# A second rounding moves from ScalarE to VectorE, a state update is cut into quarters of TensorE's columns, and the order of issue is written anew

## The chip, the cores and the metric

The kernel runs on one core of one Trainium2 chip. The core has five engines that run side by side and wait for each other through semaphores: TensorE (PE) for matrix products, VectorE (DVE) and ScalarE (ACT) for elementwise work, GpSimd (POOL) and SyncE (SP), which here issues the transfers. TensorE writes its results to PSUM, from where VectorE and ScalarE read them; all other tiles lie in SBUF. The metric is the device time of one execution in microseconds, the lower the better.

## The reference

Two stages in float32. The first is a gated linear attention over 4 batches, 8 heads, 768 positions and a head dimension of 40, given as a recurrence over positions:

```python
for t in range(S):
    m_new = np.maximum(f_gate[:, :, t] + m, i_gate[:, :, t])
    f_stab = np.exp(f_gate[:, :, t] + m - m_new)
    i_stab = np.exp(i_gate[:, :, t] - m_new)
    m = m_new
    C = f_stab * C + i_stab * outer(v_t, k_t)
    n = f_stab * n + i_stab * k_t
    y[:, :, t] = sigmoid(o_gate_t) * (C @ q_t) / max(|n . q_t|, 1)
```

(shapes of the broadcasts left out). Its output, laid out as 3072 tokens of 320 numbers, goes through a two-layer MLP with a hidden width of 2048:

```python
h = x @ w_in
sp = softplus(h)
g = h * erf(sp)
return g @ w_out
```

## The kernel before

**Attention.** The 768 positions are cut into 6 chunks of 128. One attention step takes one chunk of one batch, so there are 24 steps; step s has chunk s // 4 and batch s % 4. Inside a step the positions of the chunk are handled with matrix products, and what came before the chunk is carried in a state per batch (`state`, one 104-row tile: even heads in rows 0 to 39, odd heads in rows 64 to 103). `pe`, `ex`, `sel` make the decay factors (TensorE, exponential on ScalarE, causal select on GpSimd), `S` the products of k and q, `w` their product with the factors. `ph` (L613 to L624) makes the numerators and denominators: it adds products with the state (L619) and with the chunk's own values (L623), all of them with a stationary operand cut into four slices of 32 columns. `pk` (L628 to L633) makes the update of the state: for every head one matmul with 128 rows, a stationary operand of 40 columns (the keys) and 41 moving columns (the weighted values); its result lies in rows 0 to 39 or 64 to 103 of PSUM. `sa`, `sk0`, `sk1` then scale the state and add the update on VectorE. The last chunk (steps 20 to 23) has no `pk`, `sa` or `sk`. `den`, `yg`, `y`, `tr`, `xh`, `xl` finish the step's output, transpose it and split it into a rounded part and a rest. From step 4 on, `klo` and `qlo` (L531, L539) do the same split for k and q, whose parts are stacked by transfers (`stk`). A float32 matmul shows up as two records in the profile, and so do its weight loads.

**MLP.** Products in the rounded float32 form are fast on TensorE but lose bits, so each operand is split in two (rounded value and rest) and three of the four products are added. 48 groups are worked off; a group takes 256 tokens (the steps of two batches) and 512 of the 2048 hidden columns, so each pair of steps has four groups. A group's parts: `up0` to `up3` (L817, 32 matmuls into two PSUM tiles), `a` and `hb` (L833, L827) read them on ScalarE, a chain of ScalarE functions (`a2`, `sq`, `b`, `w`: L837, L841, L846, L858) and VectorE operations (`ah`, `ab`, `wh`: L850, L854, L862) approximates the activation, and the result stands in `hb`. Then `gh` (L867) rounds `hb` into its own tile and `gl` (L872) makes the rest, `hb` minus `gh`, on VectorE. `dn0` to `dn7` (L886, L887, L889) multiply both by the output weights, 24 matmuls; after the fourth group of a token block `o0`, `o1` copy the sums out and store them. `hb`, the two work tiles, `gh` and `gl` have two buffers each, so two groups can be between `up` and `dn` on VectorE and ScalarE.

**Weights.** Both weight matrices arrive packed as 64-bit numbers and are decoded once, in the first 100 us, in 26 pieces (`decode`, L698 to L731), using the tiles of the MLP and of attention as room.

**Order.** Nothing in the kernel is a loop over time. Every part is put on a list with a due time, which is the start of its unit (a step, a group, a chunk of gates, a decoded piece) plus an offset for the part from a table (`ATT_FIRST`, `ATT_NEXT`, `ATT` for steps 0 and 1, 2 and 3, and the rest; `MLP_FIRST`, `MLP_NEXT`, `MLP`, `MLP_END` for group 0, 1 to 3, 4 to 45, 46 and 47). The list is sorted by due time (L919) and the instructions are issued in that order; each engine takes its own in that order, one after the other. Due times set only this order, they aren't times of the chip.

Of the kernel before, what the change touches and what calls it, by code (L numbers as in the profile page):

```python
# [46 lines left out]

SETUP = {'setup': -813.8827,  # L50
    'rhs0': -388.4174,
    'rhs1': -3.147,
    'sel': -262.192}
GATE = {'load': -186.9771,
    'scan': -141.2439,
    'g': -125.5882,
    'sum': -102.716,
    'exp': -93.5536,
    'part0': -68.8941,
    'part1': -61.4429,  # L60
    'part2': -57.2668,
    'rhs': -56.4504}
ATT_FIRST = {'load': -208.3528,
    'loadv': -198.2534,
    'khi': -56.4056,
    'qhi': -409.6725,
    'klo': 276.929,
    'qlo': 281.4546,
    'stk0': -218.0962,
    'stk1': 40.1164,  # L70
    'rows': -216.9163,
    'pe0': -116.0988,
    'pe1': -102.408,
    'ex0': -111.8168,
    'ex1': -96.8755,
    'sel0': -98.0918,
    'sel1': -96.6502,
    'S0': -96.3594,
    'S1': -62.8169,
    'vg0': -88.4143,  # L80
    'vg1': -92.2802,
    'w0': -75.0031,
    'w1': -56.2056,
    'th': -55.2198,
    'pq': -206.9946,
    'qa': -240.2257,
    'pk': -77.3251,
    'ph': -43.1067,
    'sa': -140.0059,
    'sk0': -67.4399,  # L90
    'sk1': -74.5887,
    'den': -36.2945,
    'yg': -37.4924,
    'y': -12.5989,
    'tr': -3.0494,
    'xh': -2.6837,
    'xl': 1.504}
ATT_NEXT = {'load': -149.0934,
    'loadv': -49.2114,
    'khi': -8.6302,  # L100
    'qhi': 90.9856,
    'klo': 33.5053,
    'qlo': -184.8211,
    'stk0': 14.6892,
    'stk1': 195.1025,
    'rows': -194.6127,
    'pe0': -78.3983,
    'pe1': -89.2505,
    'ex0': -66.02,
    'ex1': -71.4482,  # L110
    'sel0': -51.4336,
    'sel1': -67.3981,
    'S0': -67.0238,
    'S1': -35.5688,
    'vg0': -41.9021,
    'vg1': -31.4188,
    'w0': -35.7311,
    'w1': -27.6603,
    'th': -39.2487,
    'pq': -219.6827,  # L120
    'qa': -104.0043,
    'pk': -12.9812,
    'ph': 3.8011,
    'sa': -212.9552,
    'sk0': 5.0577,
    'sk1': -4.6847,
    'den': 6.0789,
    'yg': 12.8402,
    'y': 20.8014,
    'tr': 23.7301,  # L130
    'xh': 34.3967,
    'xl': 38.586}
ATT = {'load': -35.6274,
    'loadv': -44.8494,
    'khi': -27.6843,
    'qhi': -24.58,
    'klo': -24.3722,
    'qlo': -23.7744,
    'stk0': -19.1999,
    'stk1': -17.7163,  # L140
    'rows': -57.5337,
    'pe0': -18.8968,
    'pe1': -34.5401,
    'ex0': -12.4881,
    'ex1': -29.3698,
    'sel0': -6.6822,
    'sel1': -26.618,
    'S0': -10.7393,
    'S1': -4.962,
    'vg0': -5.5713,  # L150
    'vg1': -10.3348,
    'w0': -2.8802,
    'w1': -3.1066,
    'th': 5.0062,
    'pq': -28.6139,
    'qa': -22.8277,
    'pk': 3.3201,
    'ph': 3.7715,
    'sa': 19.0615,
    'sk0': 25.9894,  # L160
    'sk1': 22.7007,
    'den': 6.5626,
    'yg': 8.3629,
    'y': 9.8824,
    'tr': 13.0984,
    'xh': 17.8939,
    'xl': 18.4217}
DEC = {'val': 5.6701,
    'bits': 8.8322,
    'hi': 14.5496,  # L170
    'lo': 23.4348,
    'dif': 18.0177}
MLP_FIRST = {'up0': -18.4204,
    'up1': -16.3411,
    'up2': -12.9276,
    'up3': -11.4394,
    'hb0': -6.2952,
    'a0': -14.0994,
    'hb1': -0.8876,
    'a1': -5.4375,  # L180
    'a2': 7.3924,
    'sq': 10.0013,
    'b': 12.0363,
    'ah': 16.7161,
    'ab': 19.9043,
    'w': 27.7463,
    'wh': 32.4163,
    'gh': 37.7164,
    'gl': 38.1861,
    'dn0': 42.3165,  # L190
    'dn1': 48.7899,
    'dn2': 54.3768,
    'dn3': 65.1336,
    'dn4': 42.1446,
    'dn5': 44.8041,
    'dn6': 50.2294,
    'dn7': 62.4136,
    'o0': 242.6862,
    'o1': 100.7839}
# [152 lines left out]
def tile_mlstm_moe(  # L352
# [136 lines left out]
    def attention(s):  # L489
# [123 lines left out]
        @at('ph')  # L613
        def _():
            v.ph = psum(H, V1)
            halves = [slice(32 * i, 32 * i + 32) for i in range(4)]
            for p in range(NPR):
                for ts in halves if c > 0 else ():
                    nc.tensor.matmul(v.ph[ts, 2 * p:2 * p + 2].rearrange("p h d -> p (h d)"),  # L619
                                     v.q[0:QR, p, ts], st[0:QR, p], start=True, stop=False)  # L620
                for j in range(2):
                    for ts in halves:
                        nc.tensor.matmul(v.ph[ts, 2 * p + j], v.w[j][:, p, ts], v.v1[:, 2 * p + j],  # L623
                                         start=(c == 0), stop=(c == 0 or j == 1))  # L624

        if not last:

            @at('pk')  # L628
            def _():
                v.pk = psum(NPR, V1)  # L630
                for p in range(NPR):
                    for j in range(2):
                        nc.tensor.matmul(v.pk[64 * j:64 * j + D, p], v.kn[:, 2 * p + j], v.vg[j][:, p], start=True, stop=True)  # L633
# [230 lines left out]
        @at('gh')  # L864
        def _():
            v.gh = moe.tile([128, W], F32R, name="gh")
            nc.scalar.activation(v.gh, v.hb, AF.Copy)  # L867
# [114 lines left out]
```

## Time and profile before

| | |
|---|---|
| runs | 507.61, 510.29, 510.26 us, median 510.26 |
| profiled execution | 505.95 us, span 504.1 us |
| TensorE busy | 478.0 us, 95% of the span |
| ScalarE busy | 447.7 us, 89% |
| VectorE busy | 438.5 us, 87% |
| GpSimd busy | 82.2 us, 16% |
| TensorE's granted clock over the span | 0.997 |

In the lines of the profile each group of instructions has its line of the code, its engine and operation, the tile it writes and the tiles it reads, their shapes and how many there were; behind the first bar stand the busy time in us and the mean length of one in ns, behind the second the idle time of the engine just ahead of them and what ended it. A line of the timeline begins with the start in us and the length in us. A line of a stretch has, for each engine, the us it was busy and how many instructions started. A line of the waits has the total in us, how many there were and the longest.

### The profile page before, as it was taken

The page shows a single profiled execution, that of the slowest core. Times are in us where ns is not written, and L with a number is a line of the kernel's source. Part 1 is how long each engine was busy: PE and PEld are TensorE (multiplying, and loading weights), DVE is VectorE, ACT ScalarE, POOL GpSimd, SP SyncE. Part 2 cuts the span into 40 slices and gives each one's busy share as a digit, 9 for nine tenths or more (in the row PEclk, how much of TensorE's full clock was granted, in tenths as well). Part 3 has the DMA queues.
Part 4 walks back from the last instruction along what each step waited for, and adds up shares of the span by engine and source line. Part 5 has one row for each costly group of instructions (what it writes and reads, how often), then busy time and mean ns, then how long its engine had stood idle before and what let it go on. Part 6 is the DMA issues. An engine that isn't in the chain of part 4 may idle for free.

```text
span 504.1 us, 14051 instructions
## 1 busy us (share of the span) xinstructions
PE 478.0 (95%) x5718; PEld 447.5 (89%) x5718; DVE 438.5 (87%) x677; ACT 447.7 (89%) x714; POOL 82.2 (16%) x112
## 2 busy tenths in 40 slices
PE   2877999899999999999999999999999999999996
PEld 1644779799899999999999999999999999999996
DVE  4878899898999999999998999999998977887663
ACT  4758999998989999889989899989899989989992
POOL 3203002311121121121121121121121211110000
PEclk9999999999999999999999999999999999999999
DMA  7986533324424514515505505415415325300000
GB/s 256 291 254 162 174 110 113 126 84 132 139 62 131 156 48 144 177 26 164 155 16 179 157 25 172 143 32 170 134 52 167 118 70 169 94 16 13 2 27 26
DMA packets 28315, 59.06 MB, mean 117 GB/s; under 512 B 4156, under 2 KB 8764, under 8 KB 28252
## 3 DMA queue, kind: packets, MB, share of 16 engines
q1 hardware_dynamic: 28252, 58.18, 38.0%
q8 instruction: 45, 0.74, 0.6%
q14 instruction: 18, 0.15, 0.1%
HBM read 33.40 MB, written 3.93 MB: 74 GB/s over the span
## 4 chain that ended last, share of the span: by engine, by line
PE 72%; ACT 12%; DVE 10%; issue 3%; DMA 2%; SPq 0%; POOL 0%; DVEq 0%; ACTq 0%
PE h L817 29%; PE po L886 10%; PE po L889 9%; PE po L887 9%; PE pa L578 3%; PE pa L619 3%; PE pa L623 2%; DVE bits L712 2%; PE pa L558 1%; PE pa L633 1%; DMA stk<-parts 1%; PE pa L677 1%; ACT gh L867 1%; DVE bits L711 1%; ACT bits L706 1%
## 5 line engine op out<-in xcount | busy, mean ns | idle before, releaser
L817 PE MATMUL h<-xh,wh 128*128 128x256 f32 x576 | 158.9, 285 | 0.8 <-ACT hb L827 0.8
L817 PE MATMUL h<-xl,wh 128*128 128x256 f32 x576 | 156.5, 281 | 0.2 <-DVE xl L690 0.2
L886 PE MATMUL po<-woh,gh 128*128 128x320 f32 x384 | 118.2, 318 | 1.1 <-ACT gh L867 1.1
L887 PE MATMUL po<-wol,gh 128*128 128x320 f32 x384 | 114.4, 309 | 0.0
L817 PEld LDWEIGHTS h<-xh,wh 128*128 128x128 f32 x576 | 108.5, 188 | 2.8 <-ACT hb L827 1.1
L817 PEld LDWEIGHTS h<-xl,wh 128*128 128x128 f32 x576 | 108.6, 188 | 0.7 <-DVE xl L690 0.5
L817 PE MATMUL h<-xh,wl 128*128 128x256 f32 x384 | 107.7, 281 | 0.0
L889 PE MATMUL po<-woh,gl 128*128 128x320 f32 x384 | 79.2, 326 | 0.0
L569 POOL TENSOR_SCALAR_AFFINE_SELECT dm<-dm 128x512 f32<-128x512 f32 x48 | 47.2, 986 | 169.6 <-ACT dm L565 162.0
L886 PEld LDWEIGHTS po<-woh,gh 128*128 128x128 f32 x384 | 72.2, 188 | 2.4 <-ACT gh L867 1.3
L817 PEld LDWEIGHTS h<-xh,wl 128*128 128x128 f32 x384 | 72.3, 188 | 0.0
L887 PEld LDWEIGHTS po<-wol,gh 128*128 128x128 f32 x384 | 72.2, 188 | 0.0
L872 DVE TENSOR_TENSOR gl<-hb,gh 128x1024 fp32r<-128x1024 f32 x48 | 58.7, 1222 | 12.1 <-ACT gh L867 11.6
L862 DVE SCALAR_TENSOR_TENSOR hb<-n,hb 128x1024 f32<-128x1024 f32 x48 | 58.6, 1220 | 10.2 <-ACT n L858 10.0
L854 DVE SCALAR_TENSOR_TENSOR n<-n,n 128x1024 f32<-128x1024 f32 x48 | 61.6, 1284 | 4.7
L889 PEld LDWEIGHTS po<-woh,gl 128*128 128x128 f32 x384 | 61.5, 189 | 1.0
L850 DVE SCALAR_TENSOR_TENSOR n<-n,hb 128x1024 f32<-128x1024 f32 x48 | 59.6, 1241 | 3.0 <-ACT n L841 3.0
L867 ACT ACTIVATE gh<-hb 128x1024 fp32r<-128x1024 f32 x48 | 50.8, 1058 | 11.9 <-DVE hb L862 10.3
L833 ACT ACTIVATE n<-h 128x512 f32<-128x512 f32 x96 | 57.2, 596 | 1.3 <-PE h L817 1.3
L858 ACT ACTIVATE n<-n 128x1024 f32<-128x1024 f32 x48 | 51.5, 1072 | 6.2 <-DVE n L854 6.1
L827 ACT ACTIVATE hb<-h 128x512 f32<-128x512 f32 x96 | 54.5, 603 | 1.1 <-PE h L817 0.7
L837 ACT ACTIVATE n<-n 128x1024 f32<-128x1024 f32 x48 | 51.0, 1064 | 1.0
(102 smaller groups left out, 797.6 us busy)
## 6 DMA issues: line engine op xcount, KB each, us to landing
stk<-parts SPq DMA_DIRECT2D x120, 160.0 KB
kvo<-in_kvo_dram SPq DMA_DIRECT2D x24, 484.0 KB
parts<-in_w_out_dram SPq DMA_DIRECT2D x5, 960.0 KB
parts<-in_qk_dram SPq DMA_DIRECT2D x20, 208.0 KB
q_t<-in_qk_dram SPq DMA_DIRECT2D x20, 208.0 KB
out_dram<-o_sb SPq DMA_DIRECT2D x24, 160.0 KB
stk<-in_qk_dram SPq DMA_DIRECT2D x4, 416.0 KB
hb<-in_w_in_dram SPq DMA_DIRECT2D x2, 512.0 KB
```

What stands on the lines that cost most here:

```text
L817: nc.tensor.matmul(v.h[n // 2][:, n % 2 * T:(n % 2 + 1) * T], w, m, start=(q == 0), stop=(q == len(ops) - 1))
L827: nc.scalar.activation(v.hb[:, hs], v.h[i], AF.Copy)
L833: nc.scalar.activation(v.a[:, hs], v.h[i], AF.Tanh, scale=PARAMS[0], bias=PARAMS[1])
L850: nc.vector.scalar_tensor_tensor(out=v.a, in0=v.a, scalar=PARAMS[8], in1=v.hb, op0=ALU.add, op1=ALU.mult)
L854: nc.vector.scalar_tensor_tensor(out=v.a, in0=v.a, scalar=PARAMS[9], in1=v.b, op0=ALU.mult, op1=ALU.add)
L858: nc.scalar.activation(v.a, v.a, AF.Tanh, scale=PARAMS[10], bias=PARAMS[11])
L862: nc.vector.scalar_tensor_tensor(out=v.hb, in0=v.a, scalar=1.0, in1=v.hb, op0=ALU.add, op1=ALU.mult)
L867: nc.scalar.activation(v.gh, v.hb, AF.Copy)
L872: nc.vector.tensor_tensor(v.gl, v.hb, v.gh.bitcast(F32), op=ALU.subtract)
L886: nc.tensor.matmul(po[k, b], v.gh[:, ts], woh[:, w], start=(j == 0), stop=False)
L887: nc.tensor.matmul(po[k, b], v.gh[:, ts], wol[:, w], start=False, stop=False)
L889: nc.tensor.matmul(po[k, b], v.gl[:, ts], woh[:, w], start=False, stop=(j == NFF - 1))
```

## The change

Three things. `gh` is written by a copy on VectorE instead of ScalarE. `pk` makes each head's update in two matmuls, one for the first 32 of the 40 key columns and one for the last 8, so that the four pieces of a pair of heads lie in four different quarters of TensorE's columns. And all the tables of due times are replaced. The code, and the lines of the tables for the parts named above (old and new values; all other entries and unit starts change likewise):

```diff
         @at('ph')
         def _():
             v.ph = psum(H, V1)
-            halves = [slice(32 * i, 32 * i + 32) for i in range(4)]
+            quarters = [slice(32 * i, 32 * i + 32) for i in range(4)]
...
                 v.pk = psum(NPR, V1)
                 for p in range(NPR):
-                    for j in range(2):
-                        nc.tensor.matmul(v.pk[64 * j:64 * j + D, p], v.kn[:, 2 * p + j], v.vg[j][:, p], start=True, stop=True)
+                    for d in (slice(0, 32), slice(32, D)):
+                        for j in range(2):
+                            nc.tensor.matmul(v.pk[64 * j + d.start:64 * j + d.stop, p], v.kn[:, 2 * p + j, d], v.vg[j][:, p],
+                                             start=True, stop=True)
...
         @at('gh')
         def _():
             v.gh = moe.tile([128, W], F32R, name="gh")
-            nc.scalar.activation(v.gh, v.hb, AF.Copy)
+            nc.vector.tensor_copy(v.gh, v.hb)
...
 ATT = {
-    'pk': 3.3201,
-    'ph': 3.7715,
+    'pk': 5.626,
+    'ph': 5.7311,
...
 MLP = {
-    'ah': 27.915,
-    'ab': 27.9988,
-    'w': 31.9713,
-    'wh': 35.0478,
-    'gh': 38.5408,
-    'gl': 39.3398,
+    'ah': 29.2802,
+    'ab': 31.7705,
+    'w': 36.3996,
+    'wh': 37.6271,
+    'gh': 40.7584,
+    'gl': 42.2482,
...
 MLP_END = {
-    'wh': 154.2504,
-    'gh': 203.734,
-    'gl': 213.6813,
+    'wh': 182.5552,
+    'gh': 193.2624,
+    'gl': 197.238,
...
-GROUP_EVERY = 13.6751
+GROUP_EVERY = 13.9448
```

The groups 46 and 47 are 13.94 apart in the new due times, and the order inside each table decides what stands next to what on an engine. With the new tables `up2` and `up3` of a group stand ahead of `up0` and `up1` in groups 4 to 45.

More of the change, by code (lines that the diff above doesn't have):

```diff
@@ L46 @@
 RAWS = {(0, 0): 0, (0, 1): 1, (0, 2): 2, (1, 0): 3, (1, 1): 4, (2, 0): 0, (2, 1): 1, (1, 2): 2, (3, 0): 3, (3, 1): 4}
[L50 to L156, printed above, removed]
-    'pk': 3.3201,
-    'ph': 3.7715,
[L159 to L199, printed above, removed]
@@ L323 @@
-GROUP_AT = {0: 13.6829, 1: 39.891, 2: 60.8627, 3: 80.6636, 4: 86.6757, 5: 101.5639, 6: 114.4195, 7: 128.3435, 8: 142.8737}
-STEP_AT = {0: -28.9212, 1: -10.28, 2: 33.3085, 3: 50.2721, 4: 113.3159, 5: 127.2279}
-CHUNK_AT = {0: -663.0126, 1: 103.1621}
-GROUP_EVERY = 13.6751
-STEP_BEFORE = (27.6368, 15.3426)
-CHUNK_BEFORE = 1.8963
+SETUP = {'setup': -928.5203,
+    'rhs0': -613.177,
+    'rhs1': -29.7752,
+    'sel': -139.3245}
+GATE = {'load': -224.6692,
+    'scan': -149.6546,
+    'g': -125.2395,
+    'sum': -114.6638,
+    'exp': -101.2865,
+    'part0': -90.4155,
+    'part1': -62.8155,
+    'part2': -61.5663,
+    'rhs': -57.2961}
@@ new lines @@
+ATT_FIRST = {'load': -331.2339,
+    'loadv': -344.4309,
+    'khi': -120.5911,
+    'qhi': -233.1144,
+    'klo': 528.3043,
+    'qlo': 144.2014,
+    'stk0': -167.2021,
+    'stk1': -136.2594,
+    'rows': -298.8524,
+    'pe0': -123.2307,
+    'pe1': -97.1572,
+    'ex0': -120.569,
+    'ex1': -83.4473,
+    'sel0': -120.3251,
+    'sel1': -68.3484,
+    'S0': -87.5465,
+    'S1': -88.9462,
+    'vg0': -66.8815,
+    'vg1': -59.7325,
+    'w0': -59.7409,
+    'w1': -59.4943,
+    'th': -89.0495,
+    'pq': -314.5437,
+    'qa': -252.6374,
+    'pk': -57.2283,
+    'ph': -47.6956,
+    'sa': -344.6918,
+    'sk0': -44.5247,
+    'sk1': -49.3669,
+    'den': -39.4944,
+    'yg': -36.4964,
+    'y': -34.3845,
+    'tr': -28.4862,
+    'xh': -18.7034,
+    'xl': -16.7492}
@@ new lines @@
+ATT_NEXT = {'load': -80.0853,
+    'loadv': -75.632,
+    'khi': 23.4282,
+    'qhi': 190.3113,
+    'klo': 227.0614,
+    'qlo': -11.47,
+    'stk0': -340.7925,
+    'stk1': 702.0529,
+    'rows': -149.8449,
+    'pe0': -102.6535,
+    'pe1': -109.1585,
+    'ex0': -94.484,
+    'ex1': -106.0558,
+    'sel0': -58.9502,
+    'sel1': -58.3061,
+    'S0': -52.0604,
+    'S1': -55.741,
+    'vg0': -49.5721,
+    'vg1': -48.0631,
+    'w0': -37.8363,
+    'w1': -37.3776,
+    'th': -40.0196,
+    'pq': -178.6846,
+    'qa': -249.8476,
+    'pk': -43.5433,
+    'ph': -18.413,
+    'sa': -287.4488,
+    'sk0': -28.2722,
+    'sk1': -36.3723,
+    'den': -9.2432,
+    'yg': -6.0606,
+    'y': 4.9134,
+    'tr': 10.5059,
+    'xh': 16.2231,
+    'xl': 24.6696}
@@ new lines @@
+ATT = {'load': -51.8544,
+    'loadv': -26.1722,
+    'khi': -29.3743,
+    'qhi': -25.6263,
+    'klo': -21.4556,
+    'qlo': -20.1171,
+    'stk0': -14.971,
+    'stk1': -16.124,
+    'rows': -40.8363,
+    'pe0': -32.6881,
+    'pe1': -23.6677,
+    'ex0': -13.5285,
+    'ex1': -21.1839,
+    'sel0': -8.1627,
+    'sel1': -12.8695,
+    'S0': -4.3635,
+    'S1': -8.9011,
+    'vg0': -5.0316,
+    'vg1': -10.5189,
+    'w0': 0.7873,
+    'w1': -6.0905,
+    'th': -11.0704,
+    'pq': -25.1779,
+    'qa': -13.5697,
+    'pk': 5.626,
+    'ph': 5.7311,
+    'sa': 25.3811,
+    'sk0': 30.8657,
+    'sk1': 30.9972,
+    'den': 9.8444,
+    'yg': 8.3836,
+    'y': 10.5116,
+    'tr': 12.8967,
+    'xh': 14.9233,
+    'xl': 18.4193}
@@ new lines @@
+DEC = {'val': 4.934,
+    'bits': 12.8513,
+    'hi': 14.2405,
+    'lo': 24.6701,
+    'dif': 18.3684}
+MLP_FIRST = {'up0': -33.2412,
+    'up1': -21.5925,
+    'up2': -30.8229,
+    'up3': -16.4832,
+    'hb0': -20.6038,
+    'a0': -17.9568,
+    'hb1': -13.277,
+    'a1': -12.8502,
+    'a2': -6.7127,
+    'sq': 4.2608,
+    'b': 8.3221,
+    'ah': 14.5215,
+    'ab': 20.7561,
+    'w': 27.5205,
+    'wh': 35.2425,
+    'gh': 37.3163,
+    'gl': 38.8657,
+    'dn0': 37.831,
+    'dn1': 40.5103,
+    'dn2': 43.5939,
+    'dn3': 46.3097,
+    'dn4': 37.781,
+    'dn5': 46.5542,
+    'dn6': 50.0325,
+    'dn7': 51.4237,
+    'o0': 314.4614,
+    'o1': 464.4019}
@@ new lines @@
+MLP_NEXT = {'up0': -15.5056,
+    'up1': -14.8841,
+    'up2': -13.7254,
+    'up3': -7.6506,
+    'hb0': -2.4947,
+    'a0': -2.5968,
+    'hb1': 2.7199,
+    'a1': 1.32,
+    'a2': 4.4483,
+    'sq': 10.2316,
+    'b': 12.9396,
+    'ah': 14.33,
+    'ab': 20.0619,
+    'w': 22.1515,
+    'wh': 26.9934,
+    'gh': 29.2921,
+    'gl': 33.225,
+    'dn0': 32.6721,
+    'dn1': 42.3334,
+    'dn2': 45.7049,
+    'dn3': 45.772,
+    'dn4': 32.9836,
+    'dn5': 37.9451,
+    'dn6': 38.7558,
+    'dn7': 39.3316,
+    'o0': 57.8221,
+    'o1': 42.358}
@@ new lines @@
+MLP = {'up0': 5.1145,
+    'up1': 9.1868,
+    'up2': 3.8109,
+    'up3': 4.1168,
+    'hb0': 15.1333,
+    'a0': 14.8988,
+    'hb1': 17.2812,
+    'a1': 18.7318,
+    'a2': 23.0236,
+    'sq': 23.3706,
+    'b': 28.4458,
+    'ah': 29.2802,
[4 more added lines that the diff above has]
+    'gl': 42.2482,
+    'dn0': 51.7159,
+    'dn1': 52.4413,
+    'dn2': 54.849,
+    'dn3': 55.9078,
+    'dn4': 56.0741,
+    'dn5': 58.5535,
+    'dn6': 58.6195,
+    'dn7': 61.3347,
+    'o0': 63.5735,
+    'o1': 70.265}
@@ new lines @@
+MLP_END = {'up0': 2.0072,
+    'up1': 4.5781,
+    'up2': 5.9872,
+    'up3': 6.5329,
+    'hb0': 15.6252,
+    'a0': 14.3867,
+    'hb1': 24.6476,
+    'a1': 19.8713,
+    'a2': 19.9417,
+    'sq': 25.1194,
+    'b': 27.988,
+    'ah': 88.4738,
+    'ab': 97.2004,
+    'w': 97.695,
+    'wh': 182.5552,
+    'gh': 193.2624,
+    'gl': 197.238,
+    'dn0': 205.9226,
+    'dn1': 213.8546,
+    'dn2': 214.3087,
+    'dn3': 214.5545,
+    'dn4': 297.4067,
+    'dn5': 298.0492,
+    'dn6': 298.9531,
+    'dn7': 300.5958,
+    'o0': 277.4824,
+    'o1': 359.6294}
@@ new lines @@
+LOAD = {(0, 0): -333.1427,
+    (0, 1): -79.9756,
+    (0, 2): -166.6898,
+    (1, 0): -28.1903,
+    (1, 1): -127.0378,
+    (2, 0): -12.0649,
+    (2, 1): 2.2675,
+    (1, 2): -32.2837,
+    (3, 0): -170.9967,
+    (3, 1): -76.6308,
+    ('o', 0): -627.3454,
+    ('o', 3): -478.9457,
+    ('o', 6): 3.2127,
+    ('o', 9): -56.1129,
+    ('o', 12): -230.6654,
+    ('o', 15): 19.4224}
+DECODE = {('i', 0, 0): -103.7423,
+    ('i', 0, 1): -54.8351,
+    ('t', 0): -65.3981,
+    ('i', 1, 0): -10.1182,
+    ('i', 1, 1): -67.8849,
+    ('o', 0): -167.113,
+    ('o', 1): -174.1159,
+    ('o', 2): -145.6058,
+    ('o', 3): -122.2135,
+    ('i', 2, 0): 8.6447,
+    ('i', 2, 1): 14.8529,
+    ('t', 1): -13.5021,
+    ('i', 3, 0): -83.4714,
+    ('i', 3, 1): -31.1617,
+    ('o', 4): -149.4123,
+    ('o', 5): -126.2123,
+    ('o', 6): 45.9593,
+    ('o', 7): 50.9311,
+    ('o', 8): 59.2719,
+    ('o', 9): -31.1749,
+    ('o', 10): 36.9086,
+    ('o', 11): 29.6144,
+    ('o', 12): -103.0389,
+    ('o', 13): -83.6161,
+    ('o', 14): -45.5832,
+    ('o', 15): 69.6967}
@@ L331, in group_at @@
+GROUP_AT = {0: 15.4252, 1: 40.0088, 2: 58.3328, 3: 78.2519, 4: 82.944, 5: 100.075, 6: 114.9869, 7: 128.343, 8: 145.1279}
+STEP_AT = {0: -32.7155, 1: -12.8846, 2: 29.2965, 3: 56.5819, 4: 109.4769, 5: 123.9825}
+CHUNK_AT = {0: -764.7163, 1: 83.9429}
+GROUP_EVERY = 13.9448
+STEP_BEFORE = (29.9975, 17.6754)
+CHUNK_BEFORE = -8.7286
 def group_at(g):
@@ L615, in _ @@
             v.ph = psum(H, V1)
-            halves = [slice(32 * i, 32 * i + 32) for i in range(4)]
+            quarters = [slice(32 * i, 32 * i + 32) for i in range(4)]
             for p in range(NPR):
-                for ts in halves if c > 0 else ():
+                for ts in quarters if c > 0 else ():
                     nc.tensor.matmul(v.ph[ts, 2 * p:2 * p + 2].rearrange("p h d -> p (h d)"),
@@ L621, in _ @@
                 for j in range(2):
-                    for ts in halves:
+                    for ts in quarters:
                         nc.tensor.matmul(v.ph[ts, 2 * p + j], v.w[j][:, p, ts], v.v1[:, 2 * p + j],
```

114 lines of the change are left out of this document (removed).

## The prediction

> **What bounds the kernel now.** I read the busy totals of the page first, then the busy time by stretch, then the waits of VectorE in the long middle stretch.
>
> ```profile
> PE 478.0 (95%) x5718; PEld 447.5 (89%) x5718; DVE 438.5 (87%) x677; ACT 447.7 (89%) x714; POOL 82.2 (16%) x112
> ...
> PE 72%; ACT 12%; DVE 10%; issue 3%; DMA 2%; SPq 0%; POOL 0%; DVEq 0%; ACTq 0%
> ```
>
> ```profile
> core 0: us, PE busy (x) PEld busy (x) DVE busy (x) ACT busy (x) POOL busy (x), PEclk, DMA share, GB/s
> 0.00:100.00 100.00, 80.53 (x760) 61.61 (x761) 82.48 (x162) 79.99 (x159) 17.83 (x38) 0.98 0.63 186
> 100.00:382.00 282.00, 279.67 (x3725) 270.46 (x3724) 266.17 (x413) 260.25 (x400) 53.56 (x62) 1.00 0.37 114
> 382.00:456.00 74.00, 74.00 (x919) 72.23 (x918) 62.59 (x81) 70.05 (x108) 10.80 (x14) 1.00 0.34 103
> 456.00:485.00 29.00, 29.00 (x225) 29.00 (x224) 18.12 (x17) 28.00 (x39) 0.00 (x0) 1.00 0.03 9
> 485.00:504.10 19.10, 14.78 (x99) 14.16 (x98) 9.10 (x8) 9.44 (x13) 0.00 (x0) 1.00 0.07 26
> ```
>
> The stretches matter more than the totals. From 100 to 485 TensorE is the bound (279.67 of 282, then all of it). From 100 to 382, where attention steps run beside the MLP, VectorE is close behind: 266.17 of 282. After 382 it has room (62.59 of 74, 18.12 of 29), because the last chunk needs no update of the state and no further gates. Before 100 no engine is full. The whole-kernel share of 87% for VectorE hides this, and the change puts work on VectorE.
>
> ```profile
> DVE kvo L661 <- ACT den L656: 4.3, 8, 1.3
> DVE gl L872 <- ACT gh L867: 2.2, 4, 0.6
> DVE hb L862 <- ACT n L858: 1.8, 4, 0.4
> DVE n L850 <- ACT n L841: 0.7, 3, 0.2
> DVE dm L592 <- PE pa L578: 0.5, 2, 0.2
> ```
>
> These are all of VectorE's waits for others from 100 to 382: 4.3 + 2.2 + 1.8 + 0.7 + 0.5 = 9.5 us. The other idle time, 282 - 266.17 - 9.5 = 6.3 us, lies between its own dependent instructions and stays whatever the others do. So VectorE has 9.5 us to give away there.
>
> **Part 1: gh moves from ScalarE to VectorE.** What goes, and the nearest rows for what comes:
>
> ```profile
> L867 ACT ACTIVATE gh<-hb 128x1024 fp32r<-128x1024 f32 x48 | 50.8, 1058 | 11.9 <-DVE hb L862 10.3
> ```
>
> ```profile
> L457 DVE CAST spl<-x 128x384 bf16<-128x384 f32 x10 | 3.5, 351 | 0.0
> ...
> L711 DVE TENSOR_SCALAR bits<-bits 128x320 int32<-128x320 int32 x16 | 5.8, 360 | 5.1 <-ACT bits L706 5.1
> L711 DVE TENSOR_SCALAR bits<-bits 128x512 int32<-128x512 int32 x10 | 4.6, 463 | 3.5 <-ACT bits L706 3.5
> ```
>
> ```profile
> 251.23 1.21 DVE L872 TENSOR_TENSOR gl<-hb,gh 128x1024 fp32r<-128x1024 f32 x1
> 252.37 1.22 DVE L850 SCALAR_TENSOR_TENSOR n<-n,hb 128x1024 f32<-128x1024 f32 x1
> ```
>
> ScalarE loses 50.8 us. In the long stretch it isn't the bound, so nothing follows from that directly. VectorE gains 48 copies of 1024 f32 elements, SBUF to SBUF. The two forms of L711 differ by 192 elements and 103 ns, 0.54 ns an element; the same slope from L457 gives 351 + 640 x 0.54 = 697 ns, I take **0.69 us**. The nearest row of the same size, L872 at 1.21 us, reads two tensors; I take the slope of the one-input rows, since a copy has one input, and keep 1.21 as the other end. Neighbours overlap by 1.21 - (252.37 - 251.23) = 0.07 us, so one copy occupies about 0.62 us.
>
> The Trainium skill, VectorE: DVE Perf Modes, section "The TRN2 errata", gives 58 + FD/2 cycles at 0.96 GHz for such a copy, an estimate of 0.59 us; by that the sum below would be some 3 us lower, about 515 us.
>
> The first operand of gl is now made on the same engine, so the 2.2 us of waits of L872 for L867 go; they are part of the 9.5. The due times put gh between hb (L862) and gl with other work mostly between, and ah and ab (L850, L854) no longer touch in most groups; counted over six periods of four groups, instructions that directly need the one before are 26 before and 27 after, so the 6.3 us stays.
>
> Between 100 and 382 there are 31 of the moved copies (the profile shows L867 31 times there), 3 before 100 and 14 after 382. VectorE then needs 282 - 9.5 + 31 x 0.62 = **291.7 us**, against 279.67 for TensorE: VectorE becomes the bound, **9.7 us** over the old length of the stretch. After 382, 8 x 0.62 = 5.0 us fits into the 11.4 idle up to 456, and the rest into 456 to 485: nothing.
>
> How much of the 9.7 us can be absorbed? VectorE works ahead of TensorE:
>
> ```profile
> 260.60 1.22 DVE L872 TENSOR_TENSOR gl<-hb,gh 128x1024 fp32r<-128x1024 f32 x1
> ```
>
> ```profile
> 258.19 1.04 ACT L867 ACTIVATE gh<-hb 128x1024 fp32r<-128x1024 f32 x1
> ...
> 261.85 0.60 ACT L827 ACTIVATE hb<-h 128x512 f32<-128x512 f32 x1
> ...
> 264.25 0.59 ACT L827 ACTIVATE hb<-h 128x512 f32<-128x512 f32 x1
> ```
>
> ```profile
> 268.78 0.28 PE L817 MATMUL h<-xh,wh 128*128 128x256 f32 x1
> ...
> 273.10 0.39 PE L886 MATMUL po<-woh,gh 128*128 128x320 f32 x1
> ```
>
> The gh written at 258.19 is used at 273.10, a lead of 15 us. But hb has two buffers: the copy of the next-but-one group at 261.85 starts 0.03 us after gl ends (260.60 + 1.22 = 261.82), it waited for it. That group's second copy ends at 264.84, and TensorE needs the PSUM tile for the group behind at 268.78, 3.9 us later. So VectorE may fall behind by up to 3.9 us, once, before TensorE stops; I take 3. Left: 9.7 - 3 = **6.7 us**.
>
> Before 100: 3 copies, 1.8 us on an engine busy for 82.48 of 100, with work of all three engines in the chain; I take 1 us (0 to 1.8). The new order of loads, decoding and first steps there I can't price from rows; TensorE idles 19.5 us in it, and I keep 3 us either way, value 0.
>
> **Part 2: the update of the state in pieces of 32 and 8 columns.**
>
> ```profile
> 216.72 0.51 PE L633 MATMUL pa<-vg,kvo 128*40 128x41 f32 x16
> 217.16 0.35 PE L619 MATMUL pa<-state,q_t 104*32 104x82 f32 x8
> 217.33 0.33 PE L623 MATMUL pa<-kvo,dm 128*32 128x41 f32 x16
> 217.48 0.33 PE L619 MATMUL pa<-state,q_t 104*32 104x82 f32 x8
> ```
>
> The 16 records of L633 hold TensorE for 217.16 - 216.72 = 0.44 us; 16 of L623, which are 32 columns wide with the same 41 moving columns, take 217.48 - 217.33 = 0.15. The change makes 32 records; at L623's rate 0.30, a gain of 0.14 us a step. By the due times pk still stands directly ahead of ph in each of the 16 steps that use the common table, so at most 16 x 0.14 = 2.2 us. If the 8-column pieces did not pack, 32 records at 0.44/16 make 0.88 us, 7 us more over the 16 steps. In my forecast both count nothing: TensorE at 277.5 to 286.7 us stays below VectorE's 291.7 - 3 = 288.7, and after 382 no state is updated.
>
> **Part 3: the end.** Here the last two groups are waited for:
>
> ```profile
> 493.44 0.41 PE L886 MATMUL po<-woh,gh 128*128 128x320 f32 x1 [1.06 <-ACT gh L867]
> ```
>
> ```profile
> 491.02 2.44 DVE L862 SCALAR_TENSOR_TENSOR hb<-n,hb 128x1024 f32<-128x1024 f32 x2
> 493.42 2.45 DVE L872 TENSOR_TENSOR gl<-hb,gh 128x1024 fp32r<-128x1024 f32 x2
> ```
>
> The new due times give VectorE hb, gh, hb, gl, gh, gl for them. From 492.16 the first gh is there at 492.85 instead of 493.4, but the first gl at 495.1 instead of 494.65, and TensorE, 8 matmuls on, waits for that. I take 0 (-0.5 to +1).
>
> **The sum.** 6.7 + 1 = 7.7 us on the profiled execution, which took 505.95 us (span 504.1 and 1.85 around it): 513.7. The three runs shown have a median of 510.26, 4.3 above that execution, so I forecast 510.26 + 7.7 = **518 us**.
>
> The largest unknown is the meeting of VectorE and GpSimd:
>
> ```profile
> L531 DVE TENSOR_TENSOR parts<-parts x20: 679/900/1122, 92.2 to 430.0; 104x512 fp32r<-104x512 f32 x20
> ...
> L587 DVE TENSOR_TENSOR vg<-kvo,dm x40: 315/322/756, 16.7 to 367.7; 128x164 f32<-128x164 f32 x40
> ...
> L854 DVE SCALAR_TENSOR_TENSOR n<-n,n x48: 1211/1225/1661, 66.1 to 489.9; 128x1024 f32<-128x1024 f32 x48
> ```
>
> ```profile
> L854 DVE SCALAR_TENSOR_TENSOR n<-n,n 128x1024 f32<-128x1024 f32 x30 | 39.0, 1300 | 3.1
> L531 DVE TENSOR_TENSOR parts<-parts 104x512 fp32r<-104x512 f32 x14 | 12.6, 901 | 0.0
> L587 DVE TENSOR_TENSOR vg<-kvo,dm 128x164 f32<-128x164 f32 x31 | 11.5, 379 | 0.0
> ...
> L569 POOL TENSOR_SCALAR_AFFINE_SELECT dm<-dm 128x512 f32<-128x512 f32 x30 | 31.2, 1040 | 113.9 <-ACT dm L565 113.9
> ```
>
> All three lines have the same instruction in a short form and one 0.44 us longer; I read that as running into a GpSimd instruction. From 100 to 382 this costs 30 x 0.075 + 14 x 0.222 + 31 x 0.057 = 7.1 us. The new order decides afresh which ones meet: from none (-7.1) to all 30 selects of L569 (30 x 0.44 = 13.2, so +6.1). I keep today's cost.
>
> The Trainium skill, SBUF — State Buffer, section "Who interferes with whom", speaks against this change: it says that an fp32 copy on VectorE in the two-port mode and a GpSimd instruction fully block each other, so the moved copies would join the ones that meet. No run here shows a copy of that size; its price is that of rival D.
>
> **The rivals.** *A, not slower: the meetings go.* If the new order sets the selects beside VectorE work that does not suffer, VectorE needs 291.7 - 7.1 = 284.6, less the 3 us lead 281.6: 0.4 under today, with today's head 509.9 us. It decides once more than about 6.7 us of the 7.1 is gone. For it: most L854 run short (median 1225). Against: ScalarE's earlier exponentials only shift the selects, nothing separates them. *B, absorbed: the lead is really usable.* If ScalarE, 32.8 us freer in the stretch, holds the chain up more deeply than the two buffers of hb suggest, most of the 15 us lead swallows the 9.7; TensorE stays the bound and part 2 counts: 510.26 - 2.2 = 508 us. Against it stands the 0.03 us between gl and the copy behind it. *C: the copy runs at one element a cycle*, 1.21 us as L872: 31 x 0.52 = 16 us more, 534 us. The L711 and L457 rows speak against it; no row shows a copy to fp32r on VectorE. *D: the copies themselves meet GpSimd*: it is busy 53.56 of 282, 19%; 31 x 0.19 x 0.44 = 2.6 us more, 520 us, and selects that start late would add to it.
>
> **How the numbers follow.** Forecast 0.50 (513 to 522 by the head and the meetings), A 0.17, B 0.15, C 0.07, D 0.11. A measurement of this kernel can tell about 0.5%, 2.6 us, from no change. A and B lie within it or, with a better head, under it: faster 0.14, same 0.24 (with the lower edge of the forecast), slower 0.62. The range of 507 to 525 takes in A and B but for a good head, and the forecast with 5 us more of meetings; left out are C and some at both edges, about 0.17.
>
> **What the profile after would show.** Right: VectorE 97% busy or more from 100 to 382 while TensorE shows idle time there for the first time, released by ScalarE's hb or by VectorE; a COPY or CAST of 0.69 us on the gh line; ScalarE near 50 us less busy. Part 2 right: pk's 32 records in 0.3 us. Wrong: TensorE still without idle time in that stretch (A or B), or a copy of 1.2 us (C).

## The result and the profile after

The changed kernel is **slower by 1.25%**: a median of 516.04 us (four runs, 510.97 to 517.65) against 509.13 us for the kernel before on the same chip (four runs, 507.61 to 510.29), ratio 1.0125 with a 95% interval of 1.0086 to 1.0165. That is 6.9 us more, against a forecast of 7.7. The profiled execution took 516.32 us, 10.4 more than the one before; the one before was quicker than any of its four runs, so this pair overstates the loss. A second profile of the changed kernel, on another chip, took 513.66. The busy totals of the first, chain of waits and row of TensorE's granted clock:

```profile
PE 483.4 (94%) x6038; PEld 449.9 (87%) x6038; DVE 464.5 (90%) x725; ACT 403.3 (78%) x666; POOL 85.7 (17%) x112
...
PEclk9886999999999999999999999999999999999999
...
DVE 49%; PE 22%; ACT 10%; DMA 8%; issue 8%; SPq 1%; DVEq 0%; ACTq 0%
```

VectorE gained 26.0 us of work and ScalarE lost 44.4. In the chain that ended last, TensorE had 72% and VectorE 10%; now VectorE has 49% and TensorE 22%. The second line, in slices of 12.9 us, shows something new in slices 2 to 4: TensorE is granted less than its full clock there. By stretch (columns as before):

```profile
core 0: us, PE busy (x) PEld busy (x) DVE busy (x) ACT busy (x) POOL busy (x), PEclk, DMA share, GB/s
0.00:100.00 100.00, 81.46 (x814) 63.14 (x814) 82.46 (x162) 76.74 (x155) 19.73 (x36) 0.91 0.58 178
100.00:382.00 282.00, 275.13 (x3810) 263.67 (x3811) 270.60 (x429) 222.44 (x355) 50.03 (x59) 0.99 0.37 114
382.00:456.00 74.00, 73.83 (x942) 71.33 (x941) 69.79 (x94) 62.98 (x99) 15.75 (x17) 1.00 0.35 108
```

The waits of VectorE for others from 100 to 382, 9.5 us before, are now 6.3:

```profile
DVE den L667 <- ACT den L658: 3.4, 14, 0.2
DVE dm L592 <- PE pa L578: 2.7, 2, 2.2
DVE kvo L663 <- PE pa L623: 0.2, 1, 0.2
```

Windows of fixed time hold less work in a slower kernel. The same work lies between the first use of `gh` by group 4 and by group 36. The first four rows below are those uses, before and after, the others the busy times between them:

```profile
121.83 0.31 PE L886 MATMUL po<-woh,gh 128*128 128x320 f32 x1
420.33 0.39 PE L886 MATMUL po<-woh,gh 128*128 128x320 f32 x1
...
121.83:420.33 298.50, 296.89 (x3833) 287.54 (x3832) 278.95 (x422) 277.19 (x426) 58.14 (x66) 1.00 0.38 115
```

```profile
123.80 0.31 PE L888 MATMUL po<-woh,gh 128*128 128x320 f32 x1
429.06 0.31 PE L888 MATMUL po<-woh,gh 128*128 128x320 f32 x1
...
123.80:429.06 305.26, 299.61 (x4063) 286.61 (x4061) 295.10 (x456) 246.13 (x392) 57.06 (x66) 1.00 0.36 112
```

These 32 groups take 6.8 us longer. TensorE's idle time in them grew from 1.6 to 5.65 us, VectorE's shrank from 19.55 to 10.2. Only 4.0 of the 6.8 us shows as idle time of TensorE; the other 2.7 lies in its busy time, whose ends are modelled, and the trace doesn't resolve it. Measured from the profile before, the new one is 2.0 us behind at group 4, 8.7 at group 36 and 10.1 at its end.

The three parts of the change in the trace after: the copy, `pk` followed by `ph`, and one group's `gl` with the first read of `up` behind it.

```profile
L869 DVE CAST gh<-hb x48: 660/690/1007, 75.3 to 504.2; 128x1024 fp32r<-128x1024 f32 x48
...
233.09 0.50 PE L634 MATMUL pa<-vg,kvo 128*32 128x41 f32 x32
233.41 0.34 PE L619 MATMUL pa<-state,q_t 104*32 104x82 f32 x8
...
261.13 1.22 DVE L874 TENSOR_TENSOR gl<-hb,gh 128x1024 fp32r<-128x1024 f32 x1
262.38 1.09 ACT L829 ACTIVATE hb<-h 128x512 f32<-128x512 f32 x2 [1.08 <-DVE gl L874]
```

The copy has a median of 0.69 us. The 32 pieces of `pk` hold TensorE for 0.32 us instead of 0.44. ScalarE's read starts 0.03 us after `gl` ends (262.35) and had waited 1.08 us for it.

### The profile page after: what moved, and what is told of

Read it like the earlier page. It is cut to its first block, busy times and chain, and to the rows that moved or that the text cites. A ratio compares the mean times of both kernels' runs of the same rounds, so it can differ in the third digit from the quotient of the medians.

```text
span 514.2 us, 14669 instructions
## 1 busy us (share of the span) xinstructions
PE 483.4 (94%) x6038; PEld 449.9 (87%) x6038; DVE 464.5 (90%) x725; ACT 403.3 (78%) x666; POOL 85.7 (17%) x112
## 4 chain that ended last, share of the span: by engine, by line
DVE 49%; PE 22%; ACT 10%; DMA 8%; issue 8%; SPq 1%; DVEq 0%; ACTq 0%
PE h L819 8%; DVE gl L874 7%; DVE hb L864 6%; DVE n L852 6%; DVE n L856 5%; DMA stk<-parts 5%; DVE dm L592 4%; DVE gh L869 3%; PE po L888 3%; PE po L891 3%; PE po L889 3%; DMA n<-in_w_in_dram 2%; DVE bits L714 2%; DVE parts L539 2%; DVE parts L531 2%
## 5 line engine op out<-in xcount | busy, mean ns | idle before, releaser
L819 PE MATMUL h<-xh,wh 128*128 128x256 f32 x576 | 163.0, 290 | 1.6 <-ACT hb L829 1.6
L819 PE MATMUL h<-xl,wh 128*128 128x256 f32 x576 | 158.5, 282 | 0.0
L888 PE MATMUL po<-woh,gh 128*128 128x320 f32 x384 | 120.9, 325 | 3.0 <-DVE gh L869 2.2
L819 PEld LDWEIGHTS h<-xh,wh 128*128 128x128 f32 x576 | 109.9, 191 | 3.6 <-ACT hb L829 2.0
L819 PEld LDWEIGHTS h<-xl,wh 128*128 128x128 f32 x576 | 109.8, 191 | 0.1
L819 PE MATMUL h<-xh,wl 128*128 128x256 f32 x384 | 108.5, 283 | 0.0
L891 PE MATMUL po<-woh,gl 128*128 128x320 f32 x384 | 82.3, 319 | 1.3 <-DVE gl L874 1.3
L819 PEld LDWEIGHTS h<-xh,wl 128*128 128x128 f32 x384 | 73.1, 190 | 0.0
L829 ACT ACTIVATE hb<-h 128x512 f32<-128x512 f32 x96 | 54.5, 601 | 12.8 <-DVE gl L874 12.8
L864 DVE SCALAR_TENSOR_TENSOR hb<-n,hb 128x1024 f32<-128x1024 f32 x48 | 58.9, 1227 | 5.6 <-ACT n L860 5.3
L856 DVE SCALAR_TENSOR_TENSOR n<-n,n 128x1024 f32<-128x1024 f32 x48 | 58.8, 1225 | 2.3
L673 POOL COPY kvo<-kvo 128x64 f32<-128x64 f32 x24 | 18.5, 772 | 197.7 <-DVE kvo L670 154.9
```

The source lines that it names most:

```text
L819: nc.tensor.matmul(v.h[n // 2][:, n % 2 * T:(n % 2 + 1) * T], w, m, start=(q == 0), stop=(q == len(ops) - 1))
L829: nc.scalar.activation(v.hb[:, hs], v.h[i], AF.Copy)
L856: nc.vector.scalar_tensor_tensor(out=v.a, in0=v.a, scalar=PARAMS[9], in1=v.b, op0=ALU.mult, op1=ALU.add)
L864: nc.vector.scalar_tensor_tensor(out=v.hb, in0=v.a, scalar=1.0, in1=v.hb, op0=ALU.add, op1=ALU.mult)
L888: nc.tensor.matmul(po[k, b], v.gh[:, ts], woh[:, w], start=(j == 0), stop=False)
L891: nc.tensor.matmul(po[k, b], v.gl[:, ts], woh[:, w], start=False, stop=(j == NFF - 1))
```

## The experiments

Eleven runs on three chips, each beside the kernel before, whose medians there were 508.03, 507.34 and 507.9 us. Where the expectations speak of V, it is the theory of the prediction: from 100 us on VectorE is the bound, and its added work makes the loss. C there is the theory that the lower clock in the head makes it (not the prediction's rival C).

For all of them I give an account of VectorE, worked out from its rows: from the end of `gl` of the fifth group to that of the 37th (32 groups), idle gaps above 0.13 us are waits, the rest of the length is what VectorE needs. "Meetings" is by how much its instructions exceed the shortest of their line in that stretch, less 0.02 us for each as spread. All in us.

| kernel | length | need | waits | meetings |
|---|---|---|---|---|
| before | 295.4 | 282.6 | 12.7 | 9.0 |
| after | 302.6 | 298.7 | 3.9 | 8.6 |
| after, once more | 302.5 | 298.6 | 3.9 | 8.5 |
| after, more matmuls in the head | 302.5 | 298.6 | 3.9 | 8.5 |
| before, `pk` cut | 294.3 | 282.5 | 11.8 | 8.9 |
| before, `gh` alone on VectorE | 311.5 | 304.8 | 6.7 | 7.7 |
| before, a further copy on VectorE | 314.7 | 306.2 | 8.5 | 9.0 |
| after, `gh` back on ScalarE | 323.9 | 277.3 | 46.7 | 7.8 |
| the same, `pk` whole | 326.8 | 277.2 | 49.6 | 7.8 |
| before without the scaling of the state | 296.1 | 276.2 | 20.0 | 9.0 |
| after without it | 298.3 | 291.7 | 6.6 | 7.6 |
| before without GpSimd's selects | 296.5 | 273.5 | 22.9 | 0.3 |
| after without them | 295.1 | 290.7 | 4.4 | 0.5 |

### One part alone: the cut of pk

```diff
 (kernel before)
-                    for j in range(2):
-                        nc.tensor.matmul(v.pk[64 * j:64 * j + D, p], v.kn[:, 2 * p + j], v.vg[j][:, p], ...)
+                    for d in (slice(0, 32), slice(32, D)):
+                        for j in range(2):
+                            nc.tensor.matmul(v.pk[64 * j + d.start:64 * j + d.stop, p], v.kn[:, 2 * p + j, d], ...)
```

> The kernel before with the cut pk alone. V, with TensorE the bound in the old kernel: 16 steps by 0.12 to 0.14 us, 1.9 to 2.3 us faster, 507. If 8-column pieces held TensorE longer, or the drain ahead of ph stayed: 509 to 516.

505.93 us, ratio 0.9954 (0.9934 to 0.9973), 2.1 us faster. This kernel's trace shows the same 0.32 us (217.07 to 217.40) and a TensorE that is still the bound from 100 to 392:

```profile
217.07 0.50 PE L634 MATMUL pa<-vg,kvo 128*32 128x41 f32 x32
217.40 0.34 PE L619 MATMUL pa<-state,q_t 104*32 104x82 f32 x8
...
100.00:392.00 292.00, 289.39 (x4068) 280.18 (x4067) 275.86 (x427) 271.04 (x417) 54.84 (x63) 1.00 0.38 117
```

Where TensorE bounds, 16 times 0.12 us, 1.9 us, is a gain, and this kernel is the fastest of the three. The 2.1 us are the difference of two medians; the single traces show 1.1 us of it in the 32 groups (295.4 to 294.3) and 0.6 over the span.

### One part alone: gh on VectorE in the old order

```diff
 (kernel before)
-            nc.scalar.activation(v.gh, v.hb, AF.Copy)
+            nc.vector.tensor_copy(v.gh, v.hb)
```

> The kernel before with gh on VectorE alone, old tables and old pk. V: VectorE needs 9 to 10 us more than the old 282 us of that stretch, some 3 absorbed: 514 to 518 at a before of 509. O: 508 to 511.

526.52 us, ratio 1.0348 (1.0317 to 1.0379): 18.5 us slower, where 5 to 9 were expected. VectorE needs 22.2 us more in the 32 groups instead of the 16.1 of the full change. This need, 304.8 us, is 9.4 over the old length, and 6.7 us of waits stay on top of it: the 32 groups grow by 16.1. Three waits of other engines, from 100 to 390 us:

```profile
ACT n L858 <- DVE n L854: 36.3, 30, 2.6
...
ACT hb L827 <- DVE gl L872: 26.1, 22, 2.3
...
PE pa L558 <- DVE xl L690: 9.4, 8, 1.6
```

The price of the copy is right here too (its rows have a mean of 0.687 us), but the loss is about twice the sum: in the old order VectorE stands late for `w`, for the next `hb` and, through `xl`, directly for TensorE.

### The load without the move

```diff
 (kernel before; gh stays on ScalarE)
             v.gl = moe.tile([128, W], F32R, name="gl")
+            nc.vector.tensor_copy(v.gl, wh[:, 0, 0:W].bitcast(F32))
             nc.vector.tensor_tensor(v.gl, v.hb, v.gh.bitcast(F32), op=ALU.subtract)
```

> The kernel before, gh still on ScalarE, with one extra copy of 1024 elements per group on VectorE ahead of gl, which gl then overwrites: the load of the moved copy without the move. V by load alone: VectorE needs 282.6 + 32 x 0.62 = 302 us for groups 5 to 36 instead of the 295 they take, less 3 of lead, and a little in the head: 512 to 516. If moving the work off ScalarE, the dependence or the new order made the loss and not VectorE's load: 507 to 510.

531.16 us, ratio 1.0453 (1.0413 to 1.0494), again far more than expected. Nothing is taken from ScalarE here, and the added copy has the same length, yet the kernel loses even more than with `gh` moved. So work of this size on VectorE is enough for a loss; that ScalarE gave something away isn't needed to explain it. Two of the waits of ScalarE and TensorE from 100 to 390:

```profile
ACT gh L867 <- DVE hb L862: 18.9, 16, 1.9
...
PE pa L558 <- DVE xl L690: 7.5, 8, 1.6
```

The same `xl` is late in the same way. Beside the full change (+6.9), `gh` alone (+18.5) shows what the new order and the cut of `pk` are worth together with it: about 12 us.

### The new order with gh on ScalarE

```diff
 (kernel after; the second run has pk whole as well)
-            nc.vector.tensor_copy(v.gh, v.hb)
+            nc.scalar.activation(v.gh, v.hb, AF.Copy)
```

> The kernel after, with gh put back on ScalarE (new tables and cut pk kept). Theory V (VectorE became the bound from 100 to 390 us): VectorE loses 30 copies of about 0.65 us there, TensorE is again busy without idle time and saves pk's 2 us: 2 to 4 us below before (505 to 508 at a before of 509) if the new order's head is as good as the old, up to 511 if the head's half clock stays. Rival O (the new order is worse by itself): 514 to 517, as after.

> The new tables alone: gh on ScalarE and pk whole. V: as before, 508 to 513, of which what is over 509 is the head; the stretch from 100 to 390 no longer than before. O: 514 to 517.

543.66 us, ratio 1.0668 (1.063 to 1.0706), and 546.1 us, ratio 1.0715 (1.0674 to 1.0757). No theory had these numbers. The first one's trace, wait and timeline:

```profile
DVE gl L874 <- ACT gh L869: 33.8, 22, 2.7
```

```profile
233.10 1.23 DVE L864 SCALAR_TENSOR_TENSOR hb<-n,hb 128x1024 f32<-128x1024 f32 x1
234.24 0.69 DVE L592 TENSOR_TENSOR dm<-pa,dm 128x512 f32<-128x512 f32 x1
237.42 1.23 DVE L874 TENSOR_TENSOR gl<-hb,gh 128x1024 fp32r<-128x1024 f32 x1 [2.50 <-ACT gh L869]
```

```profile
235.95 0.49 ACT L688 ACTIVATE xh<-pa 128x384 fp32r<-128x384 f32 x1 [0.85 <-PE pa L679]
236.34 1.05 ACT L869 ACTIVATE gh<-hb 128x1024 fp32r<-128x1024 f32 x1
```

The new tables put `gl` close behind `hb` on VectorE, which suits a `gh` made on that engine. On ScalarE `gh` has to pass `xh` first, which waits for TensorE, and VectorE stands idle 2.50 us ahead of `gl`. So these two aren't a fair "order alone": they show that the order and the engine of `gh` belong together. Part of the loss may be TensorE's clock, which in these two traces is granted by half in two and in six spells of 3.4 us inside the long stretch; that wasn't separated. An undo with due times of its own for `gh` wasn't made.

### Is VectorE the bound? Less work for it in both kernels

```diff
 (kernels before and after: the state isn't scaled, that part of the computation is left out)
-                    nc.vector.tensor_tensor(st[0:QR], st[0:QR], v.aL[0:QR]..., op=ALU.mult)
+                    pass
```

> The kernel after with the scaling of the state left out (16 VectorE instructions of 0.49 us, 15 of them between 100 and 390 us; the state then carries wrong weights, nothing else changes). V (VectorE is the bound of that stretch): about 15 x 0.41 = 6 us shorter, no more than the 7 us by which the stretch grew: 509 to 511 at 516 for after. O (the order, or TensorE's waits for something else): within 1 us of after.

> The kernel before with the same scaling left out. V: VectorE is not the bound there and TensorE is, so within 1 us of before. If VectorE set the pace there too: 5 to 6 us shorter.

After: 510.27 us, ratio to the kernel before 1.0036 (1.0012 to 1.0061), 4.2 us less than the unchanged kernel after on the same chip (514.47), where 5 to 7 were expected. Before: 508.57 us, ratio 1.0017 (0.9997 to 1.0036), no gain. Both save nearly the same need, 7.0 and 6.4 us. In the kernel after 4.3 us of it shortens the 32 groups; in the kernel before it turns into waits, 7.3 us more of them, and the length stays. That separates the two kernels: the same instructions are free to remove in one and cost time in the other. Without the scaling the chain from state to state is shorter too, but TensorE waited for the state for only 0.6 us from 100 to 382 in the kernel after.

### The meetings with GpSimd

```diff
 (kernels before and after: the causal select is left out)
-                nc.gpsimd.affine_select(out=v.w[j], in_=v.w[j], ...)
+                pass
```

> The kernel after with GpSimd's 48 causal selects left out (the factors above the diagonal then stay in, so attention is wrong; nothing else changes). V with the meetings of VectorE and GpSimd as part of VectorE's need: the 8.5 us by which VectorE's instructions are stretched in the 32 middle groups mostly go, and with them 5 to 7 us of the time: 508 to 510 at 514.5 for after. If GpSimd does not matter for the pace: within 1 us of after.

> The kernel before with the same selects left out. V: TensorE is the bound, so within 1.5 us of before although VectorE's stretch goes here too. If the meetings cost the old kernel time: 5 us shorter.

After: 502.19 us, ratio 0.9879 (0.9838 to 0.9919). Before: 504.37 us, ratio 0.9928 (0.9904 to 0.9953). Both gain more than theory V said: the kernel before 3.5 us instead of at most 1.5, and the kernel after about 12 us instead of 5 to 7, by its ratios of 1.0125 and 1.0114 on the two other chips (unchanged, it wasn't run on this one). Two lines of VectorE, first in the kernel after, then in the kernel after without the selects:

```profile
L531 DVE TENSOR_TENSOR parts<-parts x20: 677/1123/1125, 94.0 to 439.7; 104x512 fp32r<-104x512 f32 x20
...
L869 DVE CAST gh<-hb 128x1024 fp32r<-128x1024 f32 x30 | 22.0, 733 | 0.4
```

```profile
L531 DVE TENSOR_TENSOR parts<-parts x20: 679/684/687, 87.9 to 425.8; 104x512 fp32r<-104x512 f32 x20
...
L868 DVE CAST gh<-hb 128x1024 fp32r<-128x1024 f32 x31 | 21.5, 692 | 0.5
```

The long form of L531 is gone, and the account's meetings fall from 8.6 to 0.5: the long forms do come from the selects. In the kernel after this shortens the 32 groups by 7.5 us, in the kernel before not at all (1.1 longer). It is the need that falls there, by 8.0, and not the waits (3.9 and 4.4), so it isn't a shorter chain of waits that gains. The rest lies ahead of group 4: in the traces the kernel after is 3.3 to 6.2 us earlier there than with the selects, the kernel before 2.1. TensorE's clock is granted by half for less time in these heads too (see the next experiment), and the two weren't told apart. Without the selects the change is no loss: all four runs of the changed kernel (500.40 to 502.78) lie below all ten of the other (503.74 to 506.56).

### The clock in the head

```diff
 (kernel after, in decode, ahead of the matmuls of each piece)
+            for _ in range(3):
+                nc.tensor.matmul(v.z, rhsE[0][:, 0, :], rhsE[0].rearrange("p h l -> p (h l)")[:, 0:n], start=True, stop=True)
```

> The kernel after with three extra bf16 matmuls ahead of each of the 26 decoded pieces, into the PSUM tile that the piece then overwrites; they only keep TensorE busy while it would wait in the first 90 us. Theory C (some 5 us of the loss are the half clock in the head, which the new order brings on): mean clock 0.99 or more and 511 to 513 in every run. If the half clock there costs nothing, or the extra matmuls cost as much: 516 to 520.

> The kernel after once more, for the spread of its runs. C: runs with a mean clock of 0.99 or more near 511, those at 0.98 near 516. If the time does not follow the clock: 514 to 518 whatever the clock.

With the added matmuls 513.58 us (511.80 to 516.76, where C had 511 to 513), ratio 1.0116 (1.0086 to 1.0146); the kernel after unchanged on the same chip 514.47 us, 1.0114 (1.0081 to 1.0148). The stretch from 25 to 50 us (the granted clock stands behind POOL's count) in the kernels before, after, after again, and after with more matmuls:

```profile
25.00:50.00 25.00, 19.25 (x206) 11.15 (x204) 20.42 (x43) 16.25 (x38) 3.82 (x6) 0.95 0.77 205
```

```profile
25.00:50.00 25.00, 20.81 (x233) 13.39 (x234) 22.64 (x50) 17.70 (x40) 4.44 (x6) 0.77 0.73 218
```

```profile
25.00:50.00 25.00, 19.17 (x237) 12.84 (x236) 23.46 (x52) 18.07 (x40) 4.43 (x6) 0.84 0.75 231
```

```profile
25.00:50.00 25.00, 22.91 (x329) 14.65 (x316) 23.48 (x51) 18.45 (x41) 4.79 (x7) 1.00 0.71 224
```

The added matmuls keep the clock whole, but the loss stays: that trace is 0.5 us ahead of the kernel before at group 4 and 8.3 behind at the end, and the account of its 32 groups is the same to 0.1 us. So a loss comes about without the clock, in the long stretch. The clock does take part in the spread: the trace at 0.77 reaches group 4 2.0 us behind the kernel before, the one at 0.84 0.9 us ahead of it. The unchanged kernel's one run at a mean clock of 0.997 took 509.56 us, its five at 0.982 to 0.990 took 513.66 to 515.04, and the four runs of the result are ordered alike (510.97 at 0.996, 515.75 to 517.65 at 0.975 to 0.982). That would put the clock's share at 4 to 7 us of such a run; the added matmuls may cost something themselves, so the share isn't settled. At equal clock a loss remains: on that chip the kernel before took 508.58 and 509.46 us at 0.987 to 0.990 and the kernel after 513.66 to 515.04; at 0.997 it was 506.52 to 507.34 against 509.56. That last run has a span of 507.5 us, 3.4 over the trace before; with the 7.1 us of the 32 groups and the 1.4 of the end in it, its head would have to be some 5 us quicker than the old one. This is an estimate, and no trace here shows such a head.

## Why the prediction was right, point by point

**The bound moves to VectorE: right.** TensorE had 2.3 us of idle time from 100 to 382 and now has 6.9; some of it ends with ScalarE's `hb` and with VectorE, the rest with a transfer and with GpSimd (the four longest):

```profile
PE pa L578 <- DMA stk<-parts: 2.1, 1, 2.1
PE h L819 <- ACT hb L829: 1.6, 3, 0.6
PE pa L578 <- DVE q_t L610: 1.0, 1, 1.0
PE pa L679 <- POOL kvo L673: 1.0, 2, 0.8
```

VectorE is busy 270.60 of 282, 96.0%, just under the 97% I had named. That it is the bound is shown by the pair without the scaling of the state and the pair without the selects, and that added work on it alone makes a loss by the further copy.

**The copy: right.** 0.69 us, as taken. By the formula of the Trainium skill, VectorE: DVE Perf Modes, section "The TRN2 errata", the estimate was 0.59; the trace has 0.66 for the shortest, so the measured row decides. The same section of the Trainium skill adds that this formula comes out too short and puts the fixed term at about 150 cycles instead of 58, from which I estimate (150 + 512) / 0.96 = 690 ns; the trace agrees, with a median of 690.

**The sum of the long stretch, 9.7 - 3 = 6.7 us: right in size, in part by luck.** The 31 copies that it counts are those of groups 3 to 33. From the end of `gl` of group 2 to that of group 33 VectorE takes 11.7 us longer than before (10.3 in the second profile), and from the first use of `gh` by group 2 to that by group 33 TensorE takes 7.9 longer (6.5). But 3.5 (2.5) of VectorE's lateness come with group 3 alone, which has one copy: the new order does more at this edge of the head than the sum has, and the lead takes it. In the 32 groups behind, two errors cancel. By the prediction's own numbers, 0.62 us for each copy, 19.8 for 32 groups, and all waits of VectorE gone, 12.7 in the account's window, VectorE should lose 7.1 us there. Measured were 7.2 (295.4 to 302.6). But the need rose by only 16.1: the rows at their shortest add up to 20.0 more, the overlaps of neighbours take 3.3 of it back, and meetings and own gaps a little more. And 3.9 us of waits remain, where I had none. "The 6.3 us stays" was nearly right: own gaps in that window went from 6.4 to 5.8.

**The lead absorbs 3 us: right in size, but all of it at the start.** From the end of `gl` to the group's first use there were 7.7 us at group 4 and 10.9 at group 36, now 4.8 and 7.5: 2.9 and 3.4 us less. In between it is up to 4.9 less (11.3 and 6.4 at group 20), more than the 3.9 named as the limit. So the 3 us are used up by group 4, and over the 32 groups the 7.2 us of VectorE reach TensorE as 6.8. What limits it is what the prediction named, the 0.03 us between `gl` and ScalarE's next read of `up`: in the whole kernel that read now waits 12.8 us for `gl`:

```profile
L829 ACT ACTIVATE hb<-h 128x512 f32<-128x512 f32 x96 | 54.5, 601 | 12.8 <-DVE gl L874 12.8
```

**The head, 1 us: the mechanism was missing.** I priced three copies at 1 us and left the new order at 0. In the profiles the changed kernel stands 2.0 us behind or 0.9 ahead at group 4, within the 3 us that I kept either way. What I didn't foresee is the clock in it.

**Part 2, nothing in the forecast: not contradicted.** 0.32 us where 0.30 was said; alone it brings 2.1 us, of the 2.2 that I had as its most. The kernel after with `pk` whole wasn't run, so that it is worth nothing there is argued from VectorE being the bound, not measured.

**Part 3, 0 (-0.5 to +1): a little too low.** VectorE does `hb`, `gh`, `hb`, `gl`, `gh`, `gl` for the last two groups as forecast, TensorE waits 0.84 us for the first `gl`, and from group 36 to the end the kernel loses 1.4 us more, all of it behind the first use of `gh` by group 46 (1.4 in the second profile too).

**The rivals.** A, the meetings go: no, 9.0 became 8.6. They moved: L854 (now L856) fell from a mean of 1300 to 1227 ns, L531 rose from 901 to 1035 and meets GpSimd in most of its instructions. B, the lead takes all: no, it took 3 us. C, a copy of 1.21 us: no. D, the copies meet GpSimd: yes, but at 0.04 us a copy (733 against 692 ns without selects), 1.3 us over the stretch instead of 2.6. The Trainium skill, SBUF — State Buffer, section "Who interferes with whom", has such a copy and a GpSimd instruction block each other fully; the trace agrees that they meet; the longest copy here took 1.007 us, 0.35 above the shortest, while a select took 0.985 on average, so by its length no copy waited out a whole select.

**The starting time.** The 510.26 us on which the forecast stood was a little high: with the fourth run the median is 509.13. So 518 was 2 us above the measured 516.04, 1.1 of it from there and 0.8 from the sum.

**Still open:** what in the new head lowers the clock and how much of the median it costs; where 2.7 of the 6.8 us lie inside TensorE's busy time (its weight loads are idle for 18.65 us in the 32 groups instead of 10.96, which may hide there); and what a new order made for `gh` on ScalarE would give.

## What to carry to other kernels

Judge an engine's room by the stretch in which it is needed, not by its share of the whole kernel: VectorE's 87% hid a stretch in which it had 9.5 us to give and was handed 19. Moved work needs an order made for it, and the order is then tied to it: `gh` alone cost 18.5 us, the order with `gh` left behind 36 to 38, both together 7. Try the parts of a change singly: the one small part that helps the engine which really bounds (`pk`, -2.1 us) was the only one that gained by itself.

## What the runs showed that I had not expected

- **A late engine costs more than its excess.** With `gh` alone VectorE's need is 9.4 us over the old length of the 32 groups, and they grow by 16.1, because VectorE still waits. In that trace `xl` (L690) is queued behind the MLP's work and TensorE's L558 waits for it directly, 9.4 us in 8 places. That an earlier `xl` would win this back is likely, but wasn't tried.
- **A meeting isn't as long as the other's instruction.** L531 takes 0.68 us alone and 1.12 when it meets a select of 0.985: 0.44 us more, always nearly the same.
- **The granted clock of TensorE falls in the head of this kernel.** The same matmuls (L819) followed each other at 0.22 us at 49 us and at 0.12 us at 55:

```profile
48.87 0.41 PE L819 MATMUL h<-xl,wh 128*128 128x256 f32 x1
49.09 0.41 PE L819 MATMUL h<-xh,wl 128*128 128x256 f32 x1
...
55.25 0.28 PE L819 MATMUL h<-xl,wh 128*128 128x256 f32 x1
55.37 0.28 PE L819 MATMUL h<-xh,wl 128*128 128x256 f32 x1
```

  In the traces the half-granted time was 3.4 us before, 20 in the kernel after (the last 3.4 of it from 101 to 105 us) and 10 in its second profile; with more matmuls ahead of the decoding it was gone.
- **Without the GpSimd selects the kernel before is 3.5 us faster too**, though its long stretch doesn't gain from their absence: its trace is 2.1 us early at group 4. Its clock is whole in that head, where before it is half for 3.4 us, so what the selects cost by themselves there is open.
